# Moving x through HBM in three transfers, and finishing the first layer before the state work of a unit

## The chip, the cores and the metric

The kernel runs on one core of a Trainium2 chip. The time is device microseconds from one launch, and the figure that counts is the median of the runs. The engines are named as the profile names them: PE is TensorE (matmul), PEld its weight load, DVE is VectorE, ACT is ScalarE, POOL is GpSimd, SP is SyncE, which here only starts transfers. ACT starts some transfers too, from its own in-order instruction stream.

## The reference

Two blocks follow each other, all in float32.

```python
B, H, S, D = 4, 8, 768, 48
state = zeros(B, H, D, D)
for t in range(S):
    y[:, :, t] = einsum('bhd,bhde->bhe', r_t, state + (u * k_t)[..., None] * v_t[..., None, :])
    state = w_t[..., None] * state + k_t[..., None] * v_t[..., None, :]
x = y.transpose(0, 2, 1, 3).reshape(B * S, H * D)      # 3072 x 384
h = x @ w_in                                            # 384 x 2048
out = (h * sigmoid(h)) @ w_out                          # 2048 x 384
```

## The kernel before

**Units.** The 768 tokens are cut into blocks of 128, and each block is handled for two batches at a time: 12 units, numbered 0 to 11. Inside a unit the recurrence is done as a tree over token distances (levels 0 to 6): POOL forms products of the decays (`product`, line 406) and multiplies keys with them (`grow_own` line 643, `grow_keys` line 634), DVE does the same with the queries (line 616) and writes masked scores (line 710), ACT copies odd keys (line 604) and scores (line 792), PE multiplies queries with keys (`burst`, line 692). A `burst` for levels 3 and 4 stands in the middle of a unit, one for levels 5 and 6 near its end.

**The end of a unit.** `turn_apart` (line 811, PE) transposes the keys, `turn_k` (line 819, ACT) copies them to `kq`; `y_state` (line 835, PE) multiplies the old state with the queries, `y_values` (line 856, PE) adds scores times values into the PSUM tiles `p_m`, and ACT copies them to `yt` (line 861). Then `turns(i + 1)` transposes decays and keys of the next unit on DVE (line 360) and starts their first `product` on POOL; `update` multiplies `kq` with the values on PE (line 896), decays the state on POOL (line 901) and adds on DVE (line 910).

**Two layers behind it.** x is `yt` in another arrangement: heads of 48 rows at 64-row places become rows of a 384-long feature axis, cut into three chunks of 128 partitions (`xt`). `move_x` (line 928) does it with ten transfers from SBUF to SBUF: six of 48 rows, two of 32, two of 16. The first layer (`first_layer`, line 1065) computes its product by a seven-multiplication scheme in two halves of eight named pieces; `p7`, `p3` and `p4` of the second half are its last three steps, each 32 matmuls of 64 x 128 weights by 128 columns. For `p7` and `p3` DVE adds the PSUM result to what is kept (line 1077) and ACT applies the SiLU (line 1080); for `p4` ACT applies it straight from PSUM (line 1082). `sums` (line 1127, DVE, four instructions for a half) combines the results for the second layer, which is also seven products, `quarter` 0 to 6 (line 1156, PE; ACT copies at line 1161, DVE adds at line 1164).

**The order.** It is written out by hand: nothing is rescheduled, and each engine runs its instructions in that order. From unit 3 on, `mix(i)` gives the work of unit i as groups, and the loop puts steps of the two layers between them: after each group as many steps as `room` says. The 15 steps are the seven quarters of unit i - 2 and the eight first-layer steps of unit i - 1. For i of 4 and more there are eleven groups; group 0 turns the queries, group 4 holds the first burst, group 8 the second, group 9 (`end[0]`) the first POOL products of the next unit's bonus (lines 491), group 10 (`end[1]`) the end of the unit as above. Transfers started by SP (the next units' tokens, lines 127, 140, 147 and 157, and the output, line 1170) stand in the groups too; SP runs behind the other engines. Each transfer takes one of eight completion semaphores in turn, whichever engine starts it, and waits until the previous transfer of that semaphore has landed.

For units 3 to 10 the ten transfers of x are on ACT in the next unit's groups 0 (two) and 1 (eight), with a quarter's ACT copy between them; those of units 2 and 11 are on SP.

Of the kernel before, what the change touches and what calls it, by code (L numbers as in the profile page):

```python
# [8 lines left out]
F32 = mybir.dt.float32  # L9
# [29 lines left out]
def kernel(  # L39
# [11 lines left out]
    nc = tc.nc  # L51

    B, H, S, D = r.shape
# [5 lines left out]
    PD = 64  # L59
# [3 lines left out]
    TU = NB * L  # L63
    KC, FC = DM // 128, DF // 128
# [4 lines left out]
    NPAIR = 4  # L69
# [6 lines left out]
    pt = ctx.enter_context(tc.tile_pool(name="pt", bufs=2))  # L76
# [108 lines left out]
    scratch = ctx.enter_context(tc.tile_pool(name="scratch", bufs=2, space=bass.MemoryType.DRAM))  # L185
# [109 lines left out]
    room = pt.tile([128, 4, DM // 2], F32, name="partial", bufs=1).rearrange("p x d -> p (x d)")  # L295
# [27 lines left out]
    first = {}  # L323
    for l in range(NL):
        c, ni = 1 << l, L >> (l + 1)
# [18 lines left out]
    tw, tr, tk, diag, kq, xt = {}, {}, {}, {}, {}, {}  # L344
# [18 lines left out]
    turned = {}  # L363
# [91 lines left out]
    at = 768  # L455
# [365 lines left out]
    p_yt, p_kv, yt = {}, {}, {}  # L821
# [89 lines left out]
            else:  # L911
                (nc.scalar.copy if i == 0 else nc.vector.tensor_copy)(out=new, in_=p_kv[i][rows])

    def move_x(i, first=0, last=None, queue=nc.sync):

        if i not in xt:
            xt[i] = pt.tile([128, KC, TU], F32, name="xt", bufs=1)
        moves = []
        for h in range(H):
            at = h * D  # L920
            while at < (h + 1) * D:
                end = min((h + 1) * D, (at // 128 + 1) * 128)
                row = PD * (h % 2) + at - h * D
                moves.append((xt[i][at % 128:at % 128 + end - at, at // 128, :],
                              yt[i][row:row + end - at, h // 2].rearrange("p b t -> p (b t)")))
                at = end
        for to, have in moves[first:last]:
            queue.dma_start(out=to, in_=have)

    def both(fn, i, *args):  # L930
        return [(fn, i, b, *args) for b in range(NB)]

    def block_loads(i, names="wkr"):
        return [(load_blocks, i, name, g) for name in names for g in range(4)]
# [3 lines left out]
    def mix(i):  # L938

        ahead = i + 1 < len(units)  # L940

        def at(now, *steps):
            return steps if now else ()

        def bonus_steps(j, *steps):
            return [(block_bonus, j, x) for x in steps]

        def sum_steps(j, *steps):
            return [(block_sum, j, x) for x in steps]

        def turns(j):
            return [*both(turn, j, "w"), (product, j, 0), *both(turn, j, "k")]

        def start(j):
            return [*[(product, j, l) for l in range(1, NL)], (grow_own, j, 1)]

        end = [[*at(ahead, *bonus_steps(i + 1, 0, 1, 2, 3))],
               [*at(i < len(units) - NB, (turn_apart, i), (turn_k, i)), (y_state, i), *both(y_values, i), *at(ahead, *turns(i + 1)),
                (sums, i - 1, FH // 2 - 2 if i - 1 < NFAST else 0), *both(update, i), *at(not ahead, (move_x, i))]]
        if i < NPAIR:  # L960
            groups = [[*both(turn, i, "w"), (product, i, 0)],
                      [*both(turn, i, "k"), (odd_ones, i)], [*both(turn, i, "r"), (start_levels, i), (prepare_keys, i, 1)],
                      [(prepare, i, 1), *[(product, i, l) for l in range(1, NL)]],
                      [(burst, i, 1), (keep_level, i, 1)],
                      [(keep_level, i, 2), (go_on, i, 2)],
                      [(prepare, i, 3), (reverse_v, i), (bonus, i, 0), (bonus_sum, i, 0)],
                      [(bonus, i, 1), (burst, i, 3), (keep_level, i, 3), (bonus, i, 2)],
                      [(keep_level, i, 4), (go_on, i, 4), (bonus_sum, i, 1), (load_rk, i + 1), (load_u,)],
                      [(prepare, i, 5), (make_block_mask,), (bonus_spread, i), (bonus_write, i)],
                      [(burst, i, 5), (keep_level, i, 5), (keep_level, i, 6), (go_on, i, 6)], *end]  # L970
        else:
            groups = [[*both(turn, i, "r"), (grow_own, i, 0), (move_x, i - 1, 0, 2, nc.scalar)],
                      [*start(i), *sum_steps(i, 0, 1), *bonus_steps(i, 4, 5), (move_x, i - 1, 2, None, nc.scalar)],
                      [(odd_keys, i, 2), (grow_keys, i, 2, False), (grow_queries, i, 2), *sum_steps(i, 2)],
                      [(prepare, i, 3), *bonus_steps(i, 6, 7)],
                      [(burst, i, 3), (keep_level, i, 3), *sum_steps(i, 3, 4), (block_move, i), *at(ahead, (load_rk, i + 1))],
                      [(keep_level, i, 4), (go_on, i, 4)],
                      [(prepare, i, 5), (reverse_v, i)],
                      [(block_spread, i), (block_write, i)],
                      [(burst, i, 5), (keep_level, i, 5), (keep_level, i, 6), (go_on, i, 6)], *end]  # L980

        loads = [*at(i >= NPAIR and ahead, *block_loads(i + 1, "w")), *at(i >= NPAIR - 1 and ahead, *block_loads(i + 1, "r")),
                 *at(i + NSLOT < len(units), *block_loads(i + NSLOT, "k"))]
        if i + 1 < len(units):
            loads.insert(len(loads) // 2, (load_values, i + 1))

        if i == NPAIR - 1:
            late.extend(loads[-2:])
            loads = loads[:-2]
        if i == NPAIR:  # L990
            groups[1] += late
            groups[3] += loads[:2]
            loads = loads[2:]

        behind = groups[8 if i < NPAIR else 5 if i == NPAIR else 2:][:4 if i + NSLOT >= len(units) else None]
        for at, group in enumerate(behind):
            group += loads[at * len(loads) // len(behind):(at + 1) * len(loads) // len(behind)]
        return groups
# [3 lines left out]
    FH, DH = FC // 2, DM // 2  # L1002
    NFAST = 3
# [39 lines left out]
    def keep_banks():  # L1043

        for x in range(2):
            kept[f"h{x}"] = ps.tile([128, 512], F32, name="p_h", bufs=2)
            kept[f"o{x}"] = second[0].tile([128, 512], F32, name="p_o", bufs=2)
# [124 lines left out]
    def ups(i):  # L1172

        if i >= NFAST:
            order = (((0, "p1"), (0, "p5"), (0, "p2")), ((0, "p6"), (0, "n1"), (1, "p1")), ((0, "p7"), (0, "p3")),
                     ((0, "p4"), (1, "p2"), (1, "p6")), ((1, "p5"), (1, "n1")), ((1, "p7"),), ((1, "p3"),), ((1, "p4"),))
            made = [[(first_layer, i, half, name) for half, name in step] for step in order]
            if i == len(units) - 1:
                made[6].append((sums, i, 0))
            made[-1].append((sums, i, 1))  # L1180
            return made
        steps = [[(up, i, m)] for m in range(FC // 2)]
        for m in range(FH // 2 - (1 if i == len(units) - 1 else 2)):

            steps[FH // 2 + 1 + m].append((sums, i, m))
        steps[-1].append((sums, i, FH // 2 - 1))
        return steps

    def downs(i):
        return [[(quarter, i, x)] for x in range(7)]  # L1190

    def do(*steps):
        for fn, *args in steps:
            fn(*args)
# [69 lines left out]
    for i in range(3, len(units)):  # L1264
        steps = downs(i - 2) + ups(i - 1)
        groups = mix(i)
        if i - 1 >= NFAST:
            groups[3].append((sums_of_x, i - 1))
        if i == NTOK + 1:
            groups[4].insert(1, (weight_sums, 3))  # L1270
            for which, place in enumerate((6, 8, 9)):
                groups[place].append((in_weight_sums, which))
        if i == NFAST + 1:
            keep_banks()
            steps[1].append((in_weight_sums, 3))
        room = (1, 1, 0, 2, 1, 1, 1, 1, 1, 2, 2, 1, 1) if i < NPAIR else (2, 1, 2, 2, 1, 1, 1, 2, 1, 1, 1)
        for group, count in zip(groups, room):
            do(*group)
            for step in steps[:count]:
                do(*step)  # L1280
            steps = steps[count:]
# [34 lines left out]
```

## Time and profile before

| what | value |
|---|---|
| runs | 588.8, 594.56, 597.63 us; median 594.56 |
| profiled execution, span | 588.6 us (nearest run 588.8) |
| PE busy | 573.7 us, 97% |
| PEld busy | 533.3 us, 91% |
| DVE / POOL / ACT busy | 455.7 / 354.1 / 264.2 us |
| granted TensorE clock | 1.000 |
| x transfers (line 928) | 100, median 0.6 us to issue on ACT, 1.8 to 2.5 us to landing |

Which of the runs the profiled execution was is not recorded; its span lies 0.2 us under the fastest run, so that run is the nearest to its own time, and 6.0 us under the median. The whole last 420 us are a repeating pattern of about 45 us for each unit, in which PE is nearly always busy. An instruction's idle time is charged to what released it last. Times in a timeline are microseconds from the start of the span; a row such as `255.24 0.86 ACT L819 COPY ... x2` is two instructions that begin at 255.24 and take 0.86 us together.

### The profile page before, as it was taken

Reading aid. Unit: us, or ns where it says so; the run is one execution under the profiler, and the core shown is the slowest. Engines: PE = TensorE matmul, PEld = TensorE weight load, DVE = VectorE, ACT = ScalarE, POOL = GpSimd, SP = SyncE. Lnnn points to the kernel's source line nnn. Section 1 sums busy time; section 2 is a strip of 40 time slices with the busy share of each in tenths; the row PEclk is TensorE's granted clock in tenths of the full one; section 3 lists DMA queues with packets and bytes.
Section 4 is the critical chain, followed back from the end, with each engine's and each line's share of the span. In section 5 each row is a group of like instructions: output and inputs, shape, how many; then the busy total and the mean of one; then the engine's idle time right before and its main releaser. Section 6 shows DMA issues by size and latency. Waiting matters only on the chain.

```text
span 588.6 us, 19384 instructions
## 1 busy us (share of the span) xinstructions
PE 573.7 (97%) x8070; PEld 533.3 (91%) x8070; DVE 455.7 (77%) x703; ACT 264.2 (45%) x582; POOL 354.1 (60%) x415
## 2 busy tenths in 40 slices
PE   8989999999999999999999999999999989999997
PEld 8767876798899989999999989999999989999997
DVE  7979789998898898787788898888678797861150
ACT  5679694431531561561561561460470462370320
POOL 5989778357768478287486496485676677500000
PEclk9999999999999999999999999999999999999999
DMA  9957785343432643544543544444354460100000
GB/s 231 311 122 195 167 244 82 47 86 70 102 68 39 133 71 53 131 66 75 114 68 60 123 62 68 105 75 73 85 100 71 95 102 27 38 7 24 28 3 26
DMA packets 203383, 53.70 MB, mean 91 GB/s; under 512 B 186784, under 2 KB 195104, under 8 KB 203296
## 3 DMA queue, kind: packets, MB, share of 16 engines
q1 hardware_dynamic: 197360, 48.73, 41.0%
q10 hardware_dynamic: 5936, 3.74, 2.4%
q8 instruction: 63, 1.03, 0.8%
q14 instruction: 24, 0.20, 0.1%
HBM read 43.21 MB, written 5.24 MB: 82 GB/s over the span
## 4 chain that ended last, share of the span: by engine, by line
PE 76%; SPq 5%; DVE 5%; POOL 4%; DMA 4%; ACT 3%; issue 1%; ACTq 1%; POOLq 0%; DVEq 0%
PE p_o L1156 26%; PE p_h L1065 16%; PE p_o L1065 8%; PE p_h L1011 8%; PE p_h L1156 4%; PE p_m L1095 4%; PE p_m L856 2%; PE p_sc L692 2%; DVE score L561 2%; SPq L127 2%; PE p_m L835 2%; DMA vq<-in_v_dram 2%; ACT score L792 2%; POOL w_in_sb L259 2%; POOL tk L634 1%
## 5 line engine op out<-in xcount | busy, mean ns | idle before, releaser
L634 POOL TENSOR_TENSOR tk<-tk,tw 128x256 f32<-128x256 f32 x128 | 91.3, 734 | 42.8 <-ACT tk L604 27.6
L491 POOL TENSOR_TENSOR ruk<-tokens_rk 128x768 f32<-128x768 f32 (+1 forms) x32 | 53.6, 1687 | 70.9 <-DVE block_sums L525 36.6
L1156 PE MATMUL p_o<-own,temps 128*128 128x192 f32 x528 | 88.8, 327 | 1.3 <-ACT partial L1161 1.3
L1156 PEld LDWEIGHTS p_o<-own,temps 128*128 128x128 f32 x528 | 86.0, 190 | 2.5 <-ACT partial L1161 2.4
L1011 PE MATMUL p_h<-xt,w_in_sb 128*128 128x256 f32 x288 | 66.1, 384 | 1.7 <-POOL w_in_sb L259 1.5
L1065 PE MATMUL p_h<-xt,w_in_sb 128*64 128x128 f32 x1008 | 62.8, 274 | 0.4 <-issue 0.4
L1011 PEld LDWEIGHTS p_h<-xt,w_in_sb 128*128 128x128 f32 x288 | 53.6, 190 | 10.0 <-POOL w_in_sb L259 2.4
L1156 PE MATMUL p_o<-w_out_sb,gt 128*128 128x192 f32 x340 | 59.9, 329 | 0.2 <-DVE temps L1127 0.2
L616 DVE TENSOR_TENSOR tr<-tr,tw 128x512 f32<-128x512 f32 x61 | 57.3, 939 | 2.6 <-PE p_m L692 2.1
L1065 PEld LDWEIGHTS p_h<-xt,w_in_sb 128*64 128x64 f32 x1008 | 55.8, 137 | 2.0 <-issue 0.9
L1156 PEld LDWEIGHTS p_o<-w_out_sb,gt 128*128 128x128 f32 x340 | 55.3, 190 | 2.0 <-issue 1.2
L1161 ACT COPY partial<-p_o 128x192 f32<-128x192 f32 x33 | 10.6, 320 | 95.7 <-PE p_o L1156 46.5
L406 POOL TENSOR_TENSOR tw<-tw 128x256 f32<-128x256 f32 (+6 forms) x83 | 40.0, 482 | 17.7 <-DVE tw L360 13.8
L1065 PE MATMUL p_o<-xt,w_in_sb 128*64 128x128 f32 x720 | 46.9, 273 | 0.0
L604 ACT COPY tk<-tk 128x256 f32<-128x256 f32 x52 | 21.2, 407 | 53.8 <-POOL tk L634 49.2
L1065 PEld LDWEIGHTS p_o<-xt,w_in_sb 128*64 128x64 f32 x720 | 40.8, 137 | 0.0
L1074 ACT COPY gt<-p_h 128x512 f32<-128x512 f32 x45 | 26.2, 582 | 30.4 <-PE p_h L1065 30.4
L1080 ACT ACTIVATE gt<-gt 128x512 f32<-128x512 f32 x36 | 22.7, 631 | 34.1 <-DVE gt L1077 33.9
L710 DVE COPY_PREDICATED score<-mask,p_sc 128x512 f32<-128x512 int8 x42 | 31.3, 800 | 5.8 <-PE p_sc L692 5.5
L1077 DVE TENSOR_TENSOR gt<-p_o,gt 128x512 f32<-128x512 f32 x27 | 18.4, 683 | 19.4 <-PE p_o L1065 19.4
L1077 DVE TENSOR_TENSOR gt<-p_h,gt 128x512 f32<-128x512 f32 x27 | 18.6, 687 | 17.3 <-PE p_h L1065 16.2
L643 POOL TENSOR_TENSOR tk<-tk,tw 128x256 f32<-128x256 f32 x32 | 30.9, 986 | 0.0
(225 smaller groups left out, 1272.0 us busy)
## 6 DMA issues: line engine op xcount, KB each, us to landing
w_out_sb<-in_moe_w_in_dram SPq DMA_DIRECT2D x6, 768.0 KB, 7.1
w_out_sb<-in_moe_w_out_dram SPq DMA_DIRECT2D x4, 768.0 KB, 5.1
own<-in_moe_w_out_dram SPq DMA_DIRECT2D x4, 768.0 KB, 5.8
tokens_rk<-in_r_dram SPq DMA_DIRECT2D x8, 384.0 KB, 4.4
tokens_rk<-in_k_dram SPq DMA_DIRECT2D x8, 384.0 KB, 5.3
tokens_w<-in_w_dram SPq DMA_DIRECT2D x8, 384.0 KB, 6.4
raw<-in_w_dram SPq DMA_DIRECT2D x80, 32.0 KB, 2.3
raw<-in_k_dram SPq DMA_DIRECT2D x80, 32.0 KB, 2.1
```

The source lines that it names most:

```text
L406: engine.tensor_tensor(out=up, in0=t[:, :, 0::2], in1=t[:, :, 1::2], op=ALU.mult)
L491: mul = lambda out, one, two: nc.gpsimd.tensor_tensor(out=out, in0=one, in1=two, op=ALU.mult)
L616: nc.vector.tensor_tensor(out=odd, in0=odd, in1=tw[i][l][:, :, 0::2][:, :, :, None].to_broadcast([128, Q, L >> (l + 1), c]), op=ALU.mult)
L634: nc.gpsimd.tensor_tensor(out=out, in0=have, in1=odd_products(i, l, b, *blocks), op=ALU.mult)
L643: nc.gpsimd.tensor_tensor(out=have, in0=have, in1=odd_products(i, l, b, [2, NP * ni]), op=ALU.mult)
L710: nc.vector.copy_predicated(out=dst, mask=masks[l][:, :, None].to_broadcast([128, NB, NP, ni, c]), data=sc[e].rearrange("p (b q) (i c) -> ...
L1011: nc.tensor.matmul(p_h[:, a, :], lhsT=w_in_sb[:, c, f * 128:(f + 1) * 128], rhs=xt[i][:, c, :], start=(c == 0), stop=(c == KC - 1))
L1065: nc.tensor.matmul(p[h:h + PD, q, :], lhsT=left[:, f:f + PD], rhs=right, start=first and n == 0 and q == 0, stop=last and n == len(pairs) ...
L1074: nc.scalar.copy(out=g(*{"p1": (0, 0), "p6": (0, 1), "p5": (1, 1)}[name]), in_=p)
L1077: nc.vector.tensor_tensor(out=to, in0=p, in1=to, op=ALU.add)
L1095: nc.tensor.matmul(po[i, b], lhsT=gt[i, f // 2][:, f % 2, b * L:(b + 1) * L], rhs=w_out_sb[:, f, :], start=(f == 0), stop=(f == FC - 1))
L1156: nc.tensor.matmul(p, lhsT=left(f), rhs=right[:, f, :], start=which in (0, 1, 3) and f == 0, stop=f == FH - 1, skip_group_check=True)
```

## The change

Two edits.

1. x goes through a DRAM tile, `turned`. `x_out` writes `yt` there with two transfers (even heads, odd heads; each 48 partitions x 4 x 1 KB), and `x_in` reads it back into `xt` with one transfer (128 partitions x 3 x 1 KB). `x_out` stands where the first two moves stood, `x_in` where the other eight stood; `x_in` waits for both of `x_out` to land.
2. For i from 4 on, the last two first-layer steps (`p3` and `p4` of the second half, with `sums(i - 1, 1)`) both follow group 9: before, `p4` and that `sums` followed group 10. `sums(i - 1, 0)` moves from inside group 10 to the start of group 9. Unit 3 keeps its order.

On PE this puts the 32 matmuls of `p4` in front of the transposes of `turn_apart` and no longer behind `update`. On DVE the run "`p7` add, `p3` add, four transposes, four `sums`, two state adds, four `sums`, query transposes" becomes "`p7` add, four `sums`, `p3` add, four `sums`, four transposes, two state adds, query transposes". On ACT `p4`'s SiLU comes before `turn_k` and the `yt` copies, and each unit has seven transfer starts fewer. POOL's order is the same.

```diff
+    turned = {}
+    def x_out(i, queue=nc.scalar):
+        turned[i] = scratch.tile([H, D, TU], F32, name="turned", bufs=2)
+        for e in range(2):
+            queue.dma_start(out=turned[i].rearrange("(p e) d t -> e d p t", e=2)[e],
+                            in_=yt[i][PD * e:PD * e + D].rearrange("p q b t -> p q (b t)"))
+    def x_in(i, queue=nc.scalar):
+        xt[i] = pt.tile([128, KC, TU], F32, name="xt", bufs=1)
+        queue.dma_start(out=xt[i], in_=turned[i].rearrange("h d t -> (h d) t").rearrange("(c p) t -> p c t", p=128))
...
-        end = [[*at(ahead, *bonus_steps(i + 1, 0, 1, 2, 3))],
+        end = [[*at(i > NFAST, (sums, i - 1, 0)), *at(ahead, *bonus_steps(i + 1, 0, 1, 2, 3))],
                [*at(i < len(units) - NB, (turn_apart, i), (turn_k, i)), (y_state, i), *both(y_values, i), *at(ahead, *turns(i + 1)),
-                (sums, i - 1, FH // 2 - 2 if i - 1 < NFAST else 0), *both(update, i), *at(not ahead, (move_x, i))]]
+                *at(i <= NFAST, (sums, i - 1, FH // 2 - 2)), *both(update, i), *at(not ahead, (move_x, i))]]
...
-            groups = [[*both(turn, i, "r"), (grow_own, i, 0), (move_x, i - 1, 0, 2, nc.scalar)],
-                      [*start(i), *sum_steps(i, 0, 1), *bonus_steps(i, 4, 5), (move_x, i - 1, 2, None, nc.scalar)],
+            groups = [[*both(turn, i, "r"), (grow_own, i, 0), (x_out, i - 1)],
+                      [*start(i), *sum_steps(i, 0, 1), *bonus_steps(i, 4, 5), (x_in, i - 1)],
...
-        room = (1, 1, 0, 2, 1, 1, 1, 1, 1, 2, 2, 1, 1) if i < NPAIR else (2, 1, 2, 2, 1, 1, 1, 2, 1, 1, 1)
+        room = (1, 1, 0, 2, 1, 1, 1, 1, 1, 2, 2, 1, 1) if i < NPAIR else (2, 1, 2, 2, 1, 1, 1, 2, 1, 2, 0)
```

More of the change, by code (lines that the diff above doesn't have):

```diff
@@ L912, in update, with move_x @@
                 (nc.scalar.copy if i == 0 else nc.vector.tensor_copy)(out=new, in_=p_kv[i][rows])
[L914 to L928, printed above, removed]
+    turned = {}
[7 more added lines that the diff above has]
+        queue.dma_start(out=xt[i], in_=turned[i].rearrange("h d t -> (h d) t").rearrange("(c p) t -> p c t", p=128))
+    def move_x(i):
+        x_out(i, nc.sync)
+        x_in(i, nc.sync)
     def both(fn, i, *args):
```

## The prediction

> **What bounds the kernel now.** I read the engine shares first: PE is busy 97% of the span, and its clock is full in every slice, so the change, which takes no matmul away, can win only what PE idles. Next, what PE's weight loads waited for from 170 us on (units 4 to 11, where the orders differ):
>
> ```profile
> PEld p_m L835 <- ACT score L792: 3.8, 7, 1.4
> PEld p_o L1156 <- ACT partial L1161: 2.4, 4, 1.1
> PEld p_sc L811 <- ACT score L792: 0.7, 2, 0.3
> ```
>
> The columns are total, number, longest. Row one: the state product writes PSUM from which ACT is still copying scores. Row two: a quarter needs a PSUM tile that ACT empties late, and ACT's own waits say why:
>
> ```profile
> ACT partial L1161 <- DMA xt<-yt: 45.4, 9, 7.6
> ```
>
> ACT stands 45.4 us behind the moves of x. Last, POOL's waits in the same stretch, which show how much the decay products have in hand:
>
> ```profile
> POOL ruk L491 <- DVE block_sums L525: 36.6, 8, 5.8
> ```
>
> That is 4.6 us a unit in which POOL, having done the first products of a unit, waits for DVE. The timeline at the end of unit 5 is what I work on:
>
> ```profile
> 252.18 0.69 DVE L1077 TENSOR_TENSOR gt<-p_h,gt 128x512 f32<-128x512 f32 x1 [0.72 <-PE p_h L1065]
> 253.85 0.69 DVE L1077 TENSOR_TENSOR gt<-p_h,gt 128x512 f32<-128x512 f32 x1 [0.98 <-PE p_h L1065]
> ...
> 254.46 1.30 DVE L360 STREAM_TRANSPOSE tw<-raw 128x512 f32<-128x512 f32 x2
> ...
> 255.24 0.86 ACT L819 COPY kq<-p_sc 128x384 f32<-128x384 f32 x2
> ...
> 255.84 1.04 POOL L406 TENSOR_TENSOR tw<-tw 128x512 f32<-128x512 f32 x1 [0.64 <-DVE tw L360]
> ...
> 256.95 0.46 PEld L896 LDWEIGHTS p_sc<-vt,kq 128*48 128x48 f32 x16
> ...
> 258.04 1.13 DVE L1127 TENSOR_TENSOR temps<-temps,gt 128x512 f32<-128x512 f32 x1
> ```
>
> The reader is to see the order on DVE (adds, transposes, sums), that POOL's first product starts as soon as the decays are turned, and that `kq` is ready 0.8 us before PE's update uses it.
>
> **Part one: x in three transfers.** Ten starts of 0.6 us become three, so ACT issues 1.8 us a unit and not 6. What ACT waits for between them changes too. Today eight of the ten stand in front of quarter 2's copy and take turns with SP's loads for eight semaphores; in unit 6 that copy came at 315.58, PE had wanted it by about 314.8. Afterwards `x_in` waits for both `x_out` to land. The trace has no such round trip of x, so by bounds: a 192 KB write to DRAM (the output rows) lands in 2.0 us, the 64 KB write of the block sums in 1.6; 384 KB read from DRAM (the tokens) land in 4.4 to 6.4 us. In unit 5 the `yt` copies end near 261.2, the two starts near 262.4, landing by 264.9 (if the writes share engines badly, doubled, 266.9); ACT is free of `x_in` at 265.5 (267.5). Quarter 2's product ends at 267.5 and its copy is wanted by 269.8, so nothing is late, and the 2.4 us of row two go. x lands by 270 to 272, at the doubled write by 274; DVE's first use of it was at 273.99 and PE's at 279.2. Without that cover each us that the round trip takes beyond about 269 would be one PE idles in each of seven units. SP shares the semaphores: of its loads one would wait for `x_in`'s landing, seven starts later (7 x 0.5 us), up to 1 us; SP already waited 6.4 us in seven for the old moves, so I cost it at nothing. At the two places where SP moves x itself (units 2 and 11) 10 x 0.6 us become 3 x 0.6 plus one landing of 2.0: 2 us less, off PE's path, as x is used more than 10 us later.
>
> The Trainium skill speaks against this part: "DMA: Bandwidth & Descriptors", in its section on the anatomy of one DMA, puts a fixed cost of about 2.0 us on each transfer, mostly completion, and calls it longest where HBM is written. The write rows above agree at 1.6 to 2.0 us. By the page two dependent transfers of 0.39 MB cost an estimated 5.8 us in sequence; by the rows 6.4 to 8.4. Either fits in front of 273.99.
>
> **Part two: the order, on PE.** The 32 matmuls of `p4` take 1.75 us and now stand in front of the transposes and the state product. The score copies that PE waited for get 1.75 us more, longer than the longest wait (1.4), so rows one and three go: 3.8 + 0.7. What is late next is the update. It needs `turn_k`, which on ACT now stands behind `p3`'s SiLU, which needs `p3`'s add, which on DVE now stands behind four sums. Unit 5: `p7`'s add ends at 252.87; two sums with a PSUM operand take 0.6 us each from start to start, the third 1.13 beside POOL, the fourth about 0.7 (POOL is through with the bonus at 255.2; with POOL idle, in unit 11, that row is 0.68). `p3`'s add runs 255.9 to 256.6, SiLUs end at 257.2 and 257.8 (0.6 each), `turn_k` at 258.7. PE reaches the update at 256.95 + 1.75 = 258.7: no stall. In units 4 and 7 DVE comes late to `p7`'s add (207.42 in unit 4, PE done with `p3` at 208.3), the same sum gives `turn_k` done at 213.6 against PE at 213.1: 0.5 us each, together 1.0.
>
> **On DVE and POOL.** The second sums wait for `p3`'s SiLU (257.2) and run while POOL has nothing, four at 0.6 to 0.7: to 259.9. Only then come the transposes: the decays are turned at 261.2, not 255.76, so POOL's first product moves 5.4 us later. What POOL issues behind it is unchanged: in unit 5 from 255.84 to 264.48, 8.6 us, hence to 269.9. It then met a wait for DVE until 268.78, so 4.3 of the 5.4 us vanish there and 1.1 is left. Behind it are the bonus products and keys that the burst needs: their last ended at 276.76, PE started the burst at 278.13, 1.37 us of slack. So unit 5 just comes out even. The state adds follow POOL's decay and end at 264.4; DVE's query transposes start at 264.45, before 264.95, so DVE itself isn't late. Over the units (POOL's lag left, slack to the burst): 1.7 and 2.8 in unit 4, 0.6 and 1.7 in unit 6, 1.3 and 2.4 in unit 7, 0 and 0.8 in unit 8, 0.2 and 0.5 in unit 9, 1.8 and 3.2 in unit 10. But PE itself arrives earlier by what it saved, about 1 us in units 4, 6, 7, 8 and 1.6 in unit 10. The burst is therefore the next bound, and I charge 1 us in all for it.
>
> **The sum.** Gain: 3.8 + 0.7 + 2.4 = 6.9 by the weight loads' idle time; by the matmuls' own idle rows for the same waits it is 2.2 + 0.4 + 1.3 = 3.9, since the two overlap. I take 5.5. Cost: 1.0 at the update, 1.0 at the burst. Net -3.5 us on a span of 588.6. The fastest run shown, 588.8, is next to this span, the median is 6.0 above; I take the same difference from the median: 591.0.
>
> **Rivals.**
> (a) *POOL's first product becomes the bound; slower.* The point is 5.7 us (4.3 of wait plus 1.4 of slack): if the decays are turned more than that later than today, each further us is one that PE idles in front of the burst, in seven units. For it: my sum stands at 5.4, and had the second sums kept the rate beside POOL (1.13 and 1.21 for the last two, not 0.68) it would be 6.4; a slower `p3` chain adds to it. At 7.2 us it is 7 x 1.5 = 10.5, less the 5.5: about 599.5. Against it: POOL has nothing to do in exactly that stretch, and DVE's whole work up to the query transposes is the same.
> (b) *The stalls only move, and nothing is left.* The burst and the update take the 5.5 us back: 594.5. For it: the slacks above are nearly all under 1.8 us.
> (c) *x's round trip holds ACT.* If the write and the semaphores of SP's loads keep `x_in` from issuing until 2 us past 269.8, row two grows to 7 x 2 = 14, less 4.5 from part two less 2 of costs: about 602. In unit 6 the old moves ran to 315.54 for the semaphores alone; against it, `x_in` needs one of them, not eight in a row.
> (d) *All of it is gained and no stall comes*: 594.56 - 6.9 = 587.7.
>
> **Chances.** Forecast 0.42, (d) 0.14, (b) 0.22, (a) 0.16, (c) 0.06. All but the far ends of (a) and (c) lie within 2% (11.9 us), which is about what a measurement of this kernel can tell from no change, its runs being 1.5% apart. A 2% gain isn't there to be had: PE's idle time in the stretch is less than that. The range goes from (d), less 2.7 for a median that falls like the faster of the runs, to (a): 585 to 599.5.
>
> **What would show it.** Right: from 170 us on the rows of line 835 and 811 behind ACT scores and of the quarters behind ACT's copy are gone or under 0.5 us; ACT's wait for moves of x falls from 45 us to under 25; POOL's wait for block sums falls from 36.6 to under 10, as its first product starts 5 to 6 us later against the end of the unit. Wrong: weight loads of the burst (line 692) waiting for POOL's keys by more than 2 us in all, or of the update for `kq` by more than 1.5; transfers from `turned` that land after DVE wants x; a DVE that is idle in front of the second sums by more than 1 us a unit.

## The result and the profile after

| | before | after |
|---|---|---|
| median (lowest to highest), us | 592.07 (588.8 to 597.63), 6 runs | 585.06 (583.78 to 587.16), 6 runs |
| profiled execution: span, us | 588.6 | 582.4 (that run's time: 584.6) |
| PE idle in the span, us | 588.6 - 573.7 = 14.9 | 582.4 - 572.0 = 10.4 |

The ratio after to before is 0.9891, with a 95% interval of 0.9858 to 0.9924: the gain is clear of the scatter of the runs, though smaller than the 2% that the prediction takes a measurement of this kernel to tell from no change. The ratios given here leave disturbed runs out, and a ratio is not exactly the quotient of the medians beside it. The forecast was 591.0 with a range of 585.0 to 599.5; the time lies at the lower edge of the range, 0.06 us inside it, and the gain, 7.0 us by the medians and 6.2 by the spans, is about twice the 3.5 forecast.

Lines behind the move of x carry numbers higher by 3 in the kernel after: the first layer is line 1068, its adds 1080, the SiLUs 1083 and 1085, the sums 1130, the quarter 1159, its copies 1164, its adds 1167.

The engine shares of the page of the kernel after:

```profile
span 582.4 us, 19225 instructions
...
PE 572.0 (98%) x8070; PEld 534.0 (92%) x8070; DVE 433.9 (75%) x703; ACT 264.4 (45%) x582; POOL 350.4 (60%) x415
```

PE does the same work and is idle 4.5 us less (the other 1.7 of the span lie in its busy time, in which the ends of matmuls are modelled). DVE's busy time fell by 21.8 us though it runs the same instructions.

What PE's weight loads waited for in the kernel after, 170 to 525 us (total, number, longest):

```profile
PEld p_sc L692 <- issue: 2.3, 12, 0.2
PEld p_m L692 <- POOL tk L634: 1.6, 2, 0.8
PEld p_sc L811 <- issue: 1.0, 6, 0.2
PEld p_sc L692 <- POOL tk L634: 0.9, 4, 0.2
PEld p_o L1159 <- DVE ob L1167: 0.4, 1, 0.4
PEld p_h L1068 <- DVE gt L1080: 0.4, 2, 0.2
```

All three rows of before are gone: the state product (line 835) and the key transposes (811) no longer wait for ACT's score copies, and no quarter waits for ACT's copy. What is new is the burst (692) waiting for POOL's keys, 2.5 us by these rows and 1.3 by the matmuls' own idle time. ACT's waits in the same stretch, the first row and the two that name a transfer:

```profile
ACT partial L1164 <- PE p_o L1159: 52.3, 20, 4.9
...
ACT partial L1164 <- DMA turned<-yt: 3.3, 2, 1.7
ACT partial L1164 <- DMA raw<-in_r_dram: 2.6, 1, 2.6
```

ACT stood 45.4 us behind the moves of x; its copies of the quarters now stand 5.9 us behind transfers and otherwise wait for PE. (In a second profile of the same kernel, taken later, the rows that name a transfer sum to 11.7.) POOL's waits:

```profile
POOL tw L406 <- DVE tw L360: 42.0, 7, 6.5
POOL ruk L491 <- DMA tokens_rk<-in_k_dram: 31.2, 7, 5.3
POOL tk L634 <- ACT tk L604: 21.9, 8, 2.7
POOL ruk L491 <- DVE block_sums L525: 9.6, 4, 3.6
```

POOL's pause has moved from the block sums (36.6 before) to the first product (line 406, 42.0): it waits for the turned decays now. The timeline at the end of unit 5, to be held against the one in the prediction:

```profile
250.54 0.69 DVE L1080 TENSOR_TENSOR gt<-p_h,gt 128x512 f32<-128x512 f32 x1 [0.72 <-PE p_h L1068]
...
252.34 0.69 DVE L1130 TENSOR_TENSOR temps<-temps,gt 128x512 f32<-128x512 f32 x1
...
253.06 1.40 DVE L1130 TENSOR_TENSOR temps<-gt,temps 128x512 f32<-128x512 f32 x1
...
254.38 0.68 DVE L1080 TENSOR_TENSOR gt<-p_h,gt 128x512 f32<-128x512 f32 x1
...
256.21 0.86 ACT L819 COPY kq<-p_sc 128x384 f32<-128x384 f32 x2
...
257.11 0.56 PE L896 MATMUL p_sc<-vt,kq 128*48 128x48 f32 x16
...
257.72 0.69 DVE L1130 TENSOR_TENSOR temps<-gt,temps 128x512 f32<-128x512 f32 x1
...
258.33 1.30 DVE L360 STREAM_TRANSPOSE tw<-raw 128x512 f32<-128x512 f32 x2
...
259.70 1.04 POOL L406 TENSOR_TENSOR tw<-tw 128x512 f32<-128x512 f32 x1 [5.79 <-DVE tw L360]
```

`kq` is ready at 257.07 and PE's update starts at 257.11: the 0.8 us that it had in hand are used to the last 0.04, and no PE time is lost. Quarter 0 starts at 257.97 here and at 259.6 before. Against that start POOL's first product lies at +1.7 us where it lay at -3.75: 5.5 us later. In units 6, 8 and 9 the shift is the same; in units 4 and 7 it is 6.9 and in unit 10 7.5, where the product lay earlier before (-5.13 and -4.36).

The start of quarter 0 is the mark by which I place the gain:

| start of quarter 0 in unit | 3 | 4 | 6 | 8 | 10 | 11 | end of span |
|---|---|---|---|---|---|---|---|
| before, us | 169.9 | 215.4 | 304.8 | 395.3 | 485.8 | 529.0 | 588.6 |
| after, us | 169.4 | 213.7 | 302.2 | 391.7 | 480.1 | 522.9 | 582.4 |
| earlier by | 0.5 | 1.7 | 2.6 | 3.6 | 5.7 | 6.1 | 6.2 |

Of the 6.2 us, 0.5 lie before unit 4, where the order is the same; the rest comes at some 0.7 us a unit in the units whose order changed.

### The profile page after: what moved, and what is told of

It reads as the page before. It is cut to its first block, busy times and chain, and to the rows that moved or that the text cites. A ratio compares the mean times of both kernels' runs of the same rounds, so it can differ in the third digit from the quotient of the medians.

```text
span 582.4 us, 19225 instructions
## 1 busy us (share of the span) xinstructions
PE 572.0 (98%) x8070; PEld 534.0 (92%) x8070; DVE 433.9 (75%) x703; ACT 264.4 (45%) x582; POOL 350.4 (60%) x415
## 4 chain that ended last, share of the span: by engine, by line
PE 81%; POOL 6%; DVE 6%; issue 3%; SPq 2%; DMA 1%; ACT 0%; DVEq 0%; POOLq 0%
PE p_o L1159 24%; PE p_h L1068 20%; PE p_o L1068 9%; PE p_h L1014 9%; PE p_h L1159 4%; PE p_m L1098 4%; PE p_sc L692 2%; POOL tk L634 2%; PE p_m L856 2%; PE p_m L835 2%; PE p_m L692 2%; SPq L127 1%; DVE score L710 1%; DMA raw<-in_r_dram 1%; POOL w_in_sb L259 1%
## 5 line engine op out<-in xcount | busy, mean ns | idle before, releaser
L634 POOL TENSOR_TENSOR tk<-tk,tw 128x256 f32<-128x256 f32 x128 | 89.8, 722 | 30.3 <-ACT tk L604 22.9
L1014 PE MATMUL p_h<-xt,w_in_sb 128*128 128x256 f32 x288 | 67.8, 391 | 0.8 <-POOL w_in_sb L259 0.6
L525 DVE TENSOR_REDUCE block_sums<-ruk 128x4 f32<-128x192 f32 (+1 forms) x48 | 24.2, 546 | 15.0 <-POOL ruk L491 15.0
L1159 PE MATMUL p_o<-w_out_sb,temps 128*128 128x192 f32 x176 | 30.4, 326 | 0.0
```

Of the source, the lines that this page charges most:

```text
L525: add = lambda out, have: nc.vector.tensor_reduce(out=out, in_=have, axis=mybir.AxisListType.X, op=ALU.add)
L634: nc.gpsimd.tensor_tensor(out=out, in0=have, in1=odd_products(i, l, b, *blocks), op=ALU.mult)
L1014: nc.tensor.matmul(p_h[:, a, :], lhsT=w_in_sb[:, c, f * 128:(f + 1) * 128], rhs=xt[i][:, c, :], start=(c == 0), stop=(c == KC - 1))
L1159: nc.tensor.matmul(p, lhsT=left(f), rhs=right[:, f, :], start=which in (0, 1, 3) and f == 0, stop=f == FH - 1, skip_group_check=True)
```

## The experiments

Two theories stood at the start. **A**: the gain comes from `p4`'s 1.75 us in front of the state product, which give ACT time for the score copies, and from x's shorter stay on ACT; the new wait of the burst is POOL's lag of 5.5 us, which took some of the gain back. **B**: the sums in front of the transposes are the gain, because DVE runs the second four of them in POOL's pause (in the timeline the same instruction takes 1.40 us at 253.06, beside POOL, and 0.69 at 257.72, while POOL does nothing). Later runs ask what makes the burst wait, how much lag POOL can bear, and how long a trip of x the kernel can bear. Three groups of kernels each share a chip and the runs of the kernel before: the transfers alone, the order alone, the sums back, and the second sums twice (median of before 592.50); half of them twice, the changed kernel again, the values' loads later, and both of the last ideas (591.15); the sums ahead with `p4` behind, and x twice through HBM (592.51).

### The transfers alone

```diff
-        end = [[*at(i > NFAST, (sums, i - 1, 0)), *at(ahead, *bonus_steps(i + 1, 0, 1, 2, 3))],
+        end = [[*at(ahead, *bonus_steps(i + 1, 0, 1, 2, 3))],
...
-                *at(i <= NFAST, (sums, i - 1, FH // 2 - 2)), *both(update, i), *at(not ahead, (move_x, i))]]
+                (sums, i - 1, FH // 2 - 2 if i - 1 < NFAST else 0), *both(update, i), *at(not ahead, (move_x, i))]]
...
-        room = (1, 1, 0, 2, 1, 1, 1, 1, 1, 2, 2, 1, 1) if i < NPAIR else (2, 1, 2, 2, 1, 1, 1, 2, 1, 2, 0)
+        room = (1, 1, 0, 2, 1, 1, 1, 1, 1, 2, 2, 1, 1) if i < NPAIR else (2, 1, 2, 2, 1, 1, 1, 2, 1, 1, 1)
```

> The order of before, x through HBM in three transfers. Theory (each part removes its own wait): the quarters' wait for ACT's copy (2.4 us of weight-load idle, 1.3 us of matmul idle in the profile of before) goes, the state product's wait for the score copies (3.8 and 0.7) stays: 1.3 to 2.4 us faster than before, ratio 0.996 to 0.998. Rival one (the order does everything): no change, and the quarters' waits were not on the path. Rival two (the ten moves also held up SP's loads, and those held up more than the rows say): 4 us faster or more, and DVE's waits for loaded tokens fall.

Measured: 590.41 us (587.77 to 593.84, 12 runs), ratio 0.9992 (0.9962 to 1.0022). The weight loads' waits, the first, third and fourth rows:

```profile
PEld p_m L835 <- ACT score L792: 2.7, 7, 0.6
...
PEld p_o L1159 <- issue: 1.2, 7, 0.2
PEld p_sc L811 <- ACT score L792: 1.1, 3, 0.4
```

The quarters' wait for ACT's copy (2.4 us before) is gone, and the rows of 835 and 811, which belong to the order, stay. So the mechanism is as told; its worth of 1.3 to 2.4 us can't be told from nothing in this comparison.

### The order alone

The ten moves are put back as in the kernel before, everything else is as after:

```diff
-            groups = [[*both(turn, i, "r"), (grow_own, i, 0), (x_out, i - 1)],
-                      [*start(i), *sum_steps(i, 0, 1), *bonus_steps(i, 4, 5), (x_in, i - 1)],
+            groups = [[*both(turn, i, "r"), (grow_own, i, 0), (move_x, i - 1, 0, 2, nc.scalar)],
+                      [*start(i), *sum_steps(i, 0, 1), *bonus_steps(i, 4, 5), (move_x, i - 1, 2, None, nc.scalar)],
```

> The new order, x in ten moves as before. Theory: the state product's waits (3.8 + 0.7 us by weight loads, 2.6 by matmuls) go, the quarters' wait for ACT's copy stays at about 2 us, and the burst's wait for POOL's keys that the changed kernel shows (2.5 by weight loads, 1.3 by matmuls) comes: 1.5 to 3.5 us faster than before, ratio 0.994 to 0.9975. Rival (x alone carries the gain): no change.

Measured: 587.32 us (586.40 to 588.49, 7 runs), ratio 0.9917 (0.9887 to 0.9947), a larger gain than expected. Its weight loads:

```profile
PEld p_h L1065 <- DVE gt L1077: 2.3, 6, 0.8
PEld p_o L1156 <- ACT partial L1161: 1.1, 1, 1.1
...
PEld p_sc L692 <- POOL tk L634: 0.5, 2, 0.2
```

Here 835 and 811 wait for ACT by 0.2 us at most, and the quarter still does, once. The first row is a wait that the prediction did not list: `p4` writes the PSUM tile that DVE's add of `p7` (line 1077) reads, so in its new place it can stand in front of that add, here by 2.3 us in six cases and by 1.1 in the matmuls' own rows. The expected wait of the burst did not come (0.5 us, and none by the matmuls), though POOL's first product lies as late as in the changed kernel, at +1.1 to +1.7 us in units 4 to 9. The new order is thus the larger part of the gain. What the ten moves cost beside the new order can be read against the next kernel, run on the same chip, which also has the sums in their old place: the two ranges of times do not meet (586.40 to 588.49 here, 583.11 to 586.30 there), 2.8 us by the medians.

### The sums back behind the transposes, `p4` ahead

```diff
-        end = [[*at(i > NFAST, (sums, i - 1, 0)), *at(ahead, *bonus_steps(i + 1, 0, 1, 2, 3))],
+        end = [[*at(ahead, *bonus_steps(i + 1, 0, 1, 2, 3))],
...
-                *at(i <= NFAST, (sums, i - 1, FH // 2 - 2)), *both(update, i), *at(not ahead, (move_x, i))]]
+                (sums, i - 1, FH // 2 - 2 if i - 1 < NFAST else 0), *both(update, i), *at(i > NFAST, (sums, i - 1, 1)), *at(not ahead, (move_x, i))]]
...
-            made[-1].append((sums, i, 1))
+            if i == len(units) - 1:
+                made[-1].append((sums, i, 1))
```

> The changed kernel with p4 of the second half still ahead, but both sums behind the transposes again (the first in front of the state adds, the second behind them, as before). Theory: p4's place alone frees the state product; with the transposes early POOL's first product starts 5.5 us earlier and the burst's waits for POOL's keys (2.5 us by weight loads, 1.3 by matmuls) go: 1 to 2 us faster than the changed kernel, some 0.986 of before. DVE's busy time rises back by about 20 us, as the sums run beside POOL again, and that costs nothing. Rival (DVE's lower busy time is what pays): slower than the changed kernel by 2 us or more.

Measured: 584.54 us (583.11 to 586.30, 6 runs), ratio 0.9870 (0.9836 to 0.9905), not to be told from the changed kernel's 585.06. From the transfers alone, on the same chip, this kernel differs in `p4`'s place only, and it is 5.9 us faster by the medians; the two ranges do not meet. POOL's first product stands 5.6 us earlier against quarter 0 than in the changed kernel. A row of its weight loads' waits, and POOL's:

```profile
PEld p_m L692 <- POOL tk L634: 1.1, 2, 0.6
```

```profile
POOL ruk L491 <- DVE block_sums L525: 36.5, 8, 6.1
...
POOL tw L406 <- DVE tw L360: 5.9, 7, 1.6
```

The pause is back at the block sums, as in the kernel before, and yet the burst waits for the same keys in the same two units (0.8 us by the matmuls' rows; the two profiles of the changed kernel have 1.3 and 0.7). The expected 1 to 2 us did not come. Two things follow: POOL's lag, which theory A charged with the burst's wait, does not make it; and theory B falls, since the same gain is had with the sums where they were. DVE is busy 445.2 us here and 433.9 after, and the time doesn't care.

### The sums ahead, `p4` behind

The changed kernel with only its `room` as before: both sums' code is as after, but `p4` and with it the second sums again follow the end of the unit.

```diff
-        room = (1, 1, 0, 2, 1, 1, 1, 1, 1, 2, 2, 1, 1) if i < NPAIR else (2, 1, 2, 2, 1, 1, 1, 2, 1, 2, 0)
+        room = (1, 1, 0, 2, 1, 1, 1, 1, 1, 2, 2, 1, 1) if i < NPAIR else (2, 1, 2, 2, 1, 1, 1, 2, 1, 1, 1)
```

> The changed kernel with p4 and the second sums back behind the end of the unit, so that only the first sums stand ahead (and x goes through HBM). Theory (p4's place is what frees the state product): its wait for the score copies is back at 3 to 4.5 us by weight loads, and the time is that of x alone with the old order, 0.996 to 1.0 of before. Rival (the sums' place brings the gain): as fast as the changed kernel, 0.987 to 0.992.

Measured: 593.23 us (592.09 to 598.18, 10 runs), ratio 1.0029 (0.9991 to 1.0066). Weight loads:

```profile
PEld p_sc L896 <- ACT kq L819: 4.0, 6, 1.6
...
PEld p_m L835 <- ACT score L792: 2.6, 7, 0.6
...
PEld p_sc L811 <- ACT score L792: 1.0, 3, 0.3
```

With the three transfers but without `p4` in front, the waits for score copies stay and the update waits for `kq`: the first sums delay `p3`'s add, hence the SiLUs, hence `turn_k`. That is the cost that the prediction saw, and here its cover is gone: in the changed kernel `p4`'s 1.75 us on PE hide it. Together with the kernel ahead of it, this leaves `p4`'s place as the edit of the order that pays.

### The second sums twice

The four instructions of the second sums are issued a second time (they write the same values again), some 2.7 us more on DVE in each of eight units, in seven of which the transposes follow:

```diff
-            made[-1].append((sums, i, 1))
+            made[-1] += [(sums, i, 1)] * (1 if i == len(units) - 1 else 2)
```

> The changed kernel with the second sums done twice (four more DVE instructions, 2.7 us, in front of the transposes, for eight units; their result is the same). Theory (POOL's first product is the next bound: the burst now starts 0.3 to 0.9 us after POOL's last key): the product starts 2.7 us later still and PE stands in front of the burst by about 2 us in each of seven units: 10 to 16 us slower than the changed kernel, and the waits of line 692 for POOL's keys rise from 2.5 to 12 us or more. Rival (PE is the bound, POOL has room): within 2 us of the changed kernel.

Measured: 593.42 us (592.76 to 595.57, 12 runs), ratio 1.0025 (1.0001 to 1.0048): 8.4 us over the changed kernel's 585.06, less than the expected 10 to 16. The matmuls' own idle time:

```profile
PE p_m L692 <- POOL tk L634: 4.8, 7, 0.7
...
PE p_o L1159 <- DVE ob L1167: 1.0, 5, 0.2
```

Now all seven units wait for POOL's keys, and quarters wait for DVE's adds. The weight loads of line 692 wait 7.4 us for those keys, not the expected 12 or more, and part of the loss is DVE itself coming late. So rival (a) of the prediction, the decay products as the bound, is real, with a smaller loss than expected; the change stops short of it.

### Half of them twice

Only the first two of those four instructions again, 1.3 us of DVE:

```diff
-    def sums(i, m):
+    def sums(i, m, steps=4):
...
-                                  (s2, s1, lower[0], ALU.subtract), (s4, upper[0], s2, ALU.subtract)):
+                                  (s2, s1, lower[0], ALU.subtract), (s4, upper[0], s2, ALU.subtract))[:steps]:
...
-            made[-1].append((sums, i, 1))
+            made[-1] += [(sums, i, 1)] + [(sums, i, 1, 2)] * (i < len(units) - 1)
```

> The changed kernel with two of the second sums' four instructions done again (1.3 us of DVE in front of the transposes, half of what the kernel with the sums done twice had; the result is the same). With 2.7 us more, the loss was 8.9 us, 1.3 us a unit, so theory (POOL's first product has a slack of about 1.3 us left, and beyond it each us is one that PE idles): at 1.3 us more nearly all is absorbed, 0 to 2 us slower than the changed kernel. Rival (no slack, the loss is proportional to what is added): 4.5 us slower.

The changed kernel was run again beside it:

> The changed kernel once more, as the base on this chip for the three that run beside it: 0.986 to 0.992 of before.

Measured: 586.05 us (584.39 to 587.33, 12 runs), ratio 0.9915 (0.9885 to 0.9944); the changed kernel on the same chip 585.04 (583.90 to 586.19, 9 runs), ratio 0.9904 (0.9872 to 0.9935). A further lag of 1.2 us (POOL's first product at +2.9 against quarter 0, not +1.7) costs 1.0 us in all, at most; one of 2.5 (the sums twice, +4.26) costs 8.4. If each us beyond the bend costs one in each of seven units, as rival (a) has it, both losses put the bend 1.1 to 1.3 beyond the change, so at about 5.5 + 1.2 = 6.7 us against the kernel before, where the prediction put 5.7.

The second profile of the changed kernel also shows how far small rows differ between two executions of one kernel. Its matmuls' waits:

```profile
PE p_h L1068 <- DVE gt L1080: 1.5, 2, 0.8
PE p_m L692 <- POOL tk L634: 0.7, 1, 0.7
```

The burst's 1.3 us are 0.7 here, and `p4` waits 1.5 us for DVE's add of `p7`, in units 4 and 5, where the first profile has nothing by the matmuls and 0.4 by the weight loads.

### The values' loads later

In units 6 and 9 of the changed kernel the burst waits for keys, and DVE's turn of the queries in unit 6 had waited itself (the timeline of the kernel after):

```profile
309.83 1.30 DVE L360 STREAM_TRANSPOSE tr<-raw 128x512 f32<-128x512 f32 x2 [2.79 <-DMA raw<-in_r_dram]
...
321.87 0.69 PE L692 MATMUL p_m<-tr,tk 48*64 48x64 f32 x32 [0.60 <-POOL tk L634]
```

SP starts eight loads of r, then five of v, then the other eight of r. The edit puts the five of v behind all of r:

```diff
-            loads.insert(len(loads) // 2, (load_values, i + 1))
+            loads.insert(8 if i > NPAIR else len(loads) // 2, (load_values, i + 1))
```

> The changed kernel with SP's load of the values behind all loads of the block queries (five transfers, about 2.5 us of starts, for units 5 and later). In the changed kernel DVE's query transposes of units 6 and 9 wait for those loads (4.9 us in three places) and in just these two units the burst waits for POOL's keys. Theory (the rest of the burst's wait comes from SP, not from the moved sums): the transposes' wait for loads falls under 2 us, the burst's waits (2.5 us by weight loads) fall under 1, and the kernel is 0.5 to 1.5 us faster than the changed kernel. Rival (the moved sums make POOL late): the burst's waits stay.

Measured: 584.79 us (584.41 to 586.37, 8 runs), ratio 0.9905 (0.9870 to 0.9939). The only row of the burst behind POOL's keys that is left among its weight loads:

```profile
PEld p_sc L692 <- POOL tk L634: 0.2, 1, 0.2
```

DVE's waits for loads of r are gone, and with them the burst's, and so it is in the next kernel. So those waits came from SP's order, not from the change in DVE's. (The 4.9 us of the expectation lie in units 6, 7 and 10; in unit 9 the trace names no releaser for the 3.3 us that the transposes stood.) The time, 0.25 us under the changed kernel on the same chip, can't be told from it: the wait rows went and their 0.7 to 1.3 us did not show.

### Both of the last ideas

The sums behind the transposes (with `p4` ahead, as in the third experiment) and the values' loads later, together:

> The kernel with both sums behind the transposes, with the later load of the values. Theory: as with the values later alone, 0.5 to 1.5 us faster than the changed kernel, and no better than that one, as the place of the sums costs nothing. Rival (the place of the sums costs too): faster than the values later alone by 1 us or more.

Measured: 584.35 us (583.51 to 585.65, 8 runs), ratio 0.9893 (0.9855 to 0.9931). It has the lowest median of all, 0.7 us under the changed kernel beside it, and the ranges overlap. I don't call it better.

### x through HBM twice

Another transfer from DRAM to DRAM stands in `x_in`, so that ACT waits for one more landing:

```diff
     def x_in(i, queue=nc.scalar):
+        again = scratch.tile([H, D, TU], F32, name="again", bufs=2)
+        queue.dma_start(out=again.rearrange("h d t -> (h d) t").rearrange("(c p) t -> p c t", p=128),
+                        in_=turned[i].rearrange("h d t -> (h d) t").rearrange("(c p) t -> p c t", p=128))
+        turned[i] = again
```

> The changed kernel with one more copy of x inside DRAM between the write and the read, so x makes a longer trip and ACT is held until it is over. In the changed kernel ACT is through with the read's start 4.2 to 8.6 us after the first quarter begins (8.1 and 8.6 in units 6 and 9), and the copy of quarter 2 must be done by 10.4. Theory (the trip has 1.5 to 6 us of room, and costs what goes beyond it): with 3.5 to 4.5 us more, units 6 and 9 lose 2 us each and units 4 and 7 a few tenths: 3 to 7 us slower than the changed kernel, all of it in the quarters' wait for ACT's copy. Rival (the trip is far from the path): within 1.5 us.

Measured: 587.76 us (586.07 to 591.83, 10 runs), ratio 0.9932 (0.9898 to 0.9966), 2.7 us over the changed kernel's medians on the other chips, under the expected 3 to 7. The profiled execution is the slowest of the ten (591.83); its matmuls' idle time (lines are higher by 5):

```profile
PE p_o L1164 <- ACT partial L1169: 3.1, 3, 1.1
PE p_h L1073 <- DVE gt L1085: 1.9, 3, 0.7
```

The quarter waits for ACT's copy in three units: those in which ACT was through with `x_in` 11.2 us or more after quarter 0 began (it ranged from 8.2 to 11.4). In the changed kernel that point comes at 4.2 to 8.6 us. The second row is `p4` behind the add of `p7` again, so the loss is not all in the quarters, where it was expected. Rival (c) is real too, and the change has about 2 us in hand against it in its latest unit.

## Why the prediction was right and where it was not

**The size: the gain.** The mis-sized term is "I take 5.5". The span lost 6.2 - 0.5 = 5.7 us from unit 4 on, net of new waits of 1.3 us by the matmuls' rows or 3.3 by the weight loads' (behind a named engine). In the same measure the gross gain is thus 7.0 or 9.0, where the rows to be removed summed to 3.9 and 6.9: more was gained than the rows held, by either. Which measure sizes a gain better can be read from all eleven profiles of changed kernels, each held against the kernel before: the fall of the weight loads' rows with a named releaser (7.1 us before, from 170 to 525) differs from the fall of the span by 0.8 us on average, that of the matmuls' rows (3.9 before) by 1.8. For the changed kernel both fall short, 3.8 and 2.6 against 6.2. So the choice of a value between the two was the error; the weight loads' rows were nearer.

**The cost at the update: 1.0 forecast, nothing found there.** For unit 5 the sum came out: `turn_k` was to end 5.83 us after `p7`'s add (258.7 less 252.87) and ended 257.07 - 251.23 = 5.84 after it. That it is so exact is luck: the third sum was to be the slow one and took 0.69, the fourth took 1.40 in place of 0.7. In unit 4 the prediction put `turn_k` 5.5 us behind the end of `p7`'s add (213.6 less 208.1) and PE's update 5.0; they came at 5.24 and 5.21. POOL is through with the bonus earlier there, and the four sums took 2.6 us, not 3.0 (207.53 to 210.15 in the trace of after). In unit 7 the premise failed, that DVE comes late to `p7`'s add: it waited 0.71 us for PE there and `kq` was in time (346.33 against 346.37). The failed step is the carrying over of one unit's sum durations to units in which POOL stands elsewhere. A late add of `p7` does cost PE something, but in front of `p4`, a wait to which the prediction gave no term: nothing by the matmuls in the first profile of the changed kernel, 1.5 us in the second.

**The cost at the burst: 1.0 forecast, 1.3 and 0.7 found, from another cause.** POOL's first product moved 5.5 us (5.4 worked out). But the wait is there with the product 5.6 us earlier, and goes when SP's loads are reordered. The failed step is "PE itself arrives earlier by what it saved", with the slacks left per unit: POOL's chain had about 1 us more slack than my rows gave (6.7 in place of 5.7), so the lag cost nothing that the runs show, while an earlier burst met loads that come no earlier. One of the prediction's signs of being wrong did appear, weight loads of the burst waiting more than 2 us for POOL's keys (2.5, and 1.5 in the second profile); the lag that it was to betray wasn't its cause.

**The base.** "The fastest run shown, 588.8, is next to this span" set the forecast at 594.56 - 3.5. In every run for which both are known the time lies 1.7 to 2.2 us above the span (584.6 and 582.4 for after). So the span of 588.6 belongs to a run of 590.3 to 590.8, and the median of six runs is 592.07, not 594.56. So about 2.5 of the forecast's error of 5.9 us is the base, a median of three runs, and 3.5 is the size of the gain. That the time still fell inside the range was in part luck: the lower edge was (d) less 2.7 us for a lower median, and the median did come out lower.

**x's trip.** ACT's 1.8 us of issue became about 1.1 (two starts of 0.33 and one of 0.42 in place of three of 0.6), its wait for moves fell from 45.4 to 5.9 us, 11.7 in the second profile (under 25 was asked), and the trip took 2.7 + 3.1 = 5.8 us from issue to landing. My bounds from rows, 6.4 to 8.4, lay above it: the write took longer than its row (2.7, not 2.0), the read less (3.1, not 4.4 to 6.4). The estimate from the Trainium skill's page "DMA: Bandwidth & Descriptors" in the prediction, 5.8, agrees with the trace; that section, on the anatomy of one DMA, gives its figure for transfers that POOL starts, while these were started by ACT. The page's warning did not tell against the change, because x is wanted later than that (at 273.99 in the stretch that the prediction works on).

**The rivals.** (d), all gained and no stall, is nearest: -6.9 worked out, -6.2 to -7.0 measured. (b), the stalls only move, is refuted by the ratio. (a) and (c) did not happen; the second sums twice and the two trips show that both mechanisms exist, 1.2 us and about 2 us further on. The doubled sums, 2.5 us further, cost 8.4, where a bend at 5.7 and 7 us of loss for each us beyond it would have made about 16: the bend lies later. (c) was priced for all seven units, and with two trips three of them were late. Its sum of 602 does not follow from its terms either: 14 of wait where there are 2.4, less 4.5, plus 2 of costs, is 603.7.

**Open.** Whether x's three transfers alone pay beside the old order (0.9962 to 1.0022) is not settled; beside the new order they do, in a comparison that also moves the sums. The burst's 0.7 to 1.3 us of waits went without the time following: what took their place wasn't found. And not all of the 7.0 us between the medians is idle time of PE. The kernels with `p4` behind the end of the unit (the one before, the transfers alone, the sums ahead) had a mean granted clock of 0.988 to 0.994 in 34 of the 89 runs for which it is known, mostly the long ones; of the 78 runs of the kernels with `p4` ahead none was under 0.996. Among runs at 0.996 and more, on the chip where both ran side by side, the median of the kernel before is 590.3 and that of the changed kernel 585.04: 5.3 us of 6.1. Why the clock gives way in one order and not in the other no run here shows.

## What to carry to other kernels

Where PE waits a little in each repetition for another engine to empty its PSUM, look for matmuls later in the order that need little of what comes before them and put them in front of the wait: 1.75 us of them removed waits of up to 1.4 us and hid a later `kq` as well. Ask what they wait for in the new place themselves: here it was the add of `p7`, up to 1.5 us. Then follow each engine that is delayed by it to the place where it last waited for something: a wait that vanishes pays for the lag first, and only what exceeds it and the slack behind it reaches the bound engine. Take the base of a forecast from several runs, and size PE's gain from its weight loads' rows rather than from the matmuls': in the eleven profiles here they came nearer to the span, though both can fall short.

## What the runs showed that I had not expected

The sums' third and fourth instructions, f32 with both operands in SBUF, run at 0.69 us with POOL idle and at 0.68 to 1.40 beside POOL. The same rows of the kernel before and of the kernel after (times in ns, minimum, median, maximum):

```profile
L1127 DVE TENSOR_TENSOR temps<-temps,gt x25: 411/1124/1237, 103.3 to 569.4; 128x512 f32<-128x512 f32 x18, 128x256 f32<-128x256 f32 x7
```

```profile
L1130 DVE TENSOR_TENSOR temps<-temps,gt x25: 413/685/1230, 102.8 to 563.3; 128x512 f32<-128x512 f32 x18, 128x256 f32<-128x256 f32 x7
```

The median fell from 1124 to 685 ns, because the second sums now fall into POOL's pause. But medians mislead here: added up, the third and fourth instructions on 512 columns fell from 37.2 to 28.5 us, and the whole line by 8.3 of the 21.8 us by which DVE's busy time fell. The larger part, 13.3 us, is the differences of x that the first layer needs (line 1039, 1042 in the kernel after; 37.3 to 24.0 us), whose 45 instructions on 128 columns took up to 1.92 us each beside POOL before. The first two durations I had seen, but not that most rows would change; it bought no time that the runs show (the kernel with the sums back is busy 445.2 us on DVE and as fast).

The starts of x's transfers got shorter, not only fewer: 0.60 us for 48 rows from SBUF to SBUF, 0.33 for 192 KB to DRAM and 0.42 for 384 KB from DRAM (the second group of the trace of after):

```profile
L926 ACTq DMA_DIRECT2D xt<-turned x8: 383/422/447, 173.2 to 484.8; - x8
...
DMA to landing us min/median/max: 3.0/3.1/3.3
```

The 384 KB landed in 3.1 us, where loads of the same size from the inputs took the 4.4 to 6.4 us that I had bounded it by.
